# Second FFN matrix converted in blocks of three feature tiles, its last quarter inside the second product; the gMLP's output rows converted in the gMLP

## The chip, the core and the metric

The kernel runs on one core of one Trainium2 chip. The core has TensorE (PE, matmuls and, as PEld, their weight loads), VectorE (DVE), ScalarE (ACT), GpSimd (POOL) and SyncE (SP), which issues all the transfers of this kernel. The metric is device time in microseconds of one execution. Three executions of the kernel before took 1011.33, 1014.9 and 1015.18 us (median 1014.9); a fourth, the profiled one, took 1010.06 us.

## The reference

Attention with capped scores, then a feed-forward layer with layer norm, then a gated MLP (gMLP), for 4 batches of 448 tokens and 768 features (12 heads of 64). The matrices come as 64-bit floats, since each was drawn as 32-bit and scaled by a 64-bit factor. Cut to what is computed:

```python
def _attn_ref(q, k, v, cap):
    scores = cap * np.tanh(scale * (q @ k.T) / cap)
    attn = softmax(scores)
    return attn @ v

def _moe_ref(x, g_ln, w_ch1, w_ch2):                 # w_ch1 768x3072, w_ch2 3072x768
    xn = (x - mu) / np.sqrt(var + 1e-06) * g_ln
    ch = np.maximum(xn @ w_ch1, 0.0) @ w_ch2
    return x + ch

def _moe2_ref(x, w_in, w_spatial, b_spatial, w_out): # w_in 768x1024, w_out 512x768
    h = np.maximum(x @ w_in, 0.0)
    u, v = h[..., :512], h[..., 512:]
    v_n = (v - mean(v)) / np.sqrt(var(v) + 1e-06)
    v_s = np.einsum('ts,bsd->btd', w_spatial, v_n) + b_spatial[None, :, None]
    return (u * v_s) @ w_out
```

## The kernel before

The four batches are worked in two passes, batches 0 and 1 first, then 2 and 3. In the first pass TensorE computes attention for batches 0 and 1 (to about 100 us), then the hidden layer of this pair beside the attention of batches 2 and 3 (`h_units`, 100 to 345 us), then the product with the second feed-forward matrix (`y_seven`, 345 to 497 us) and the gMLP (`gmlp`, from 497 us). The second pass repeats hidden layer, `y_seven` and gMLP for batches 2 and 3.

A matmul in full precision is done as three matmuls with operands split into a high and a low part: `cp` rounds a tile to the high part, `sub` subtracts it to get the low part. Every weight row and every hidden tile goes through this pair of instructions, on ScalarE or VectorE, before TensorE reads it.

Conversion of the matrices. A matrix arrives as pairs of 32-bit words. `value` loads one row of it into a raw tile and makes 32-bit floats in another tile: one ScalarE pass over the upper words (`Prelu` with a power-of-two scale), then either one ScalarE pass over the lower words and one VectorE instruction that joins both (rows of the gMLP, kinds `wv`, `wu`, `wo`), or two VectorE instructions (a shift and a join; kinds `w1`, `w2`). The row is written to DRAM (`kept`), and later uses load the kept copy. For the second matrix (`w2`) a row is one feature tile of one of six groups: 128 partitions x 512 columns, 36 rows. They are converted during the first pass's hidden layer, spread over it by `todo`, with two raw tiles of 512 pairs (`w4`).

`y_seven` computes the second feed-forward product as a 2x2 block product with seven half-size products, in the order 1, 7, 6, 4, 5, 2, 3. Each product runs over six groups; a group is 18 matmuls of 448 columns. `left_block(n, g)` gives the left operand of group g: the quarters of the matrix (a11, a12, a21, a22; three feature tiles by two 128-row tiles, 768 columns a group) come from the kept copy or are formed from others. Product 2's is a12, which product 3 reuses. The left block is split into tile `whm` in groups 0 and 4 and into the ring of three `wh` tiles in the others; there is one `whm`. Hidden tiles `hs` are loaded ahead into ten buffers and split into `rs`.

During products 4, 5 and 2 of the first pass one row of the gMLP's matrices is converted per group (`beside`, `LATER`): six `wv`, four `wu`, six `wo`, with two raw tiles (`w6m`) of 768 pairs and two result tiles (`wcm`).

The order of the work is written by a planner in the kernel itself. The whole program is recorded, each instruction gets a due time from TensorE's position and from the buffers that it frees, and `plan` picks, engine by engine, the ready instruction that is due first, up to `AHEAD` = 28 us ahead of TensorE. The result is one fixed order per engine. On the chip each engine works through its own in that order and waits at an instruction until its inputs and its buffer are there; what stands behind waits too.

Line 553 is the recorder through which nearly all instructions are issued, so tiles, not lines, tell them apart. In names of tiles: `w6m<-in_w_u_dram` is the raw load of a `wu` row, `wcm<-w6m` its first ScalarE pass, `w6m<-w6m` the second (in place over the lower words), `wcm<-wcm,w6m` the VectorE join, `kept_wu<-wcm` the write; `wc<-w` and `kept_w<-wc` belong to rows of the second matrix, `wr<-w` to those of the first (768 columns, converted with the same kinds of instruction); `wqm` and `wqs` hold loaded quarters of the second matrix.

Of the kernel before, what the change touches and what calls it, by code (L numbers as in the profile page):

```python
# [10 lines left out]
F32 = mybir.dt.float32  # L11
F32R = mybir.dt.float32r
I32 = mybir.dt.int32
U32 = mybir.dt.uint32
# [29 lines left out]
FIRST = 2, 7, 2, 10, 2, 2  # L44
# [9 lines left out]
LATER = 4, 5, 2  # L54
# [506 lines left out]
def attn_ffn_gmlp_kernel(  # L561
# [52 lines left out]
    def staged(stage, kind, n, name=None):  # L614
# [14 lines left out]
    w6, es, qks, hx, wc, w4 = (  # L629
        staged(stage, kind, n, name) for (stage, kind, name), n in zip(  # L630
            ((one, "w6", "w6"), (att, "es", "es"), (att, "qk", "qk"), (one, "acc", "hx"), (one, "wq", "wc"),
             (one, "w4", "w4")), FIRST))
# [3 lines left out]
    rbg, vsg, qkg, bsg = (staged(gate, k, n, k + "g") for k, n in (("rb", 8), ("vt", 7), ("qk", 2), ("acc", 1)))  # L636
# [11 lines left out]
    rb, raw6 = [rbg, rb3], [w6, wc, w4]  # L648
# [49 lines left out]
    kept2 = []  # L698
    made = {}
# [8 lines left out]
    def ahead(kind, j):  # L708

        with prog.early():  # L710
            value(kind, j, pool=raw6[1])

    def value(kind, j, home=None, pool=wr):

        n = width[kind]
        if kind == "ws":
            t = hs.get()
            SP.dma_start(out=t, in_=source[kind][j])
        elif (kind, j) in kept:
            t = pool.get()[:, 0:n]  # L720
            SP.dma_start(out=t, in_=kept[kind, j])
        else:
            raw = raw6[0 if n > DH else 2].get()[:, 0:n]
            SP.dma_start(out=raw.rearrange("p n t -> p (n t)"), in_=source[kind][j].bitcast(I32))
            t = pool.get()[:, 0:n]
            ti = t.bitcast(I32)
            hi, lo = raw[:, :, 1], raw[:, :, 0]
            if home is None:
                A.activation(out=t, in_=hi.bitcast(F32), func=ACTF.Prelu, scale=REBASE, alpha=-(2.0 ** 32))
            else:  # L730
                with prog.either():
                    for e in (V, A):
                        if e is A:
                            A.activation(out=t, in_=hi.bitcast(F32), func=ACTF.Copy, scale=REBASE)
                        else:
                            V.tensor_scalar(out=t, in0=hi.bitcast(F32), scalar1=REBASE, scalar2=None, op0=ALU.mult)
            if home is None and kind in ("wv", "wu", "wo"):
                A.activation(out=lo, in_=lo.bitcast(U32), func=ACTF.Copy, scale=TOP, bias=FLOOR)
                V.scalar_tensor_tensor(out=ti, in0=ti, scalar=3, in1=lo, op0=ALU.logical_shift_left,
                                       op1=ALU.bitwise_or)  # L740
            else:
                V.tensor_scalar(out=ti, in0=ti, scalar1=3, scalar2=None, op0=ALU.logical_shift_left)
                if home is not None:
                    V.scalar_tensor_tensor(out=ti, in0=hi, scalar=-(1 << 31), in1=ti, op0=ALU.bitwise_and,
                                           op1=ALU.bitwise_or)
                V.scalar_tensor_tensor(out=ti, in0=lo, scalar=29, in1=ti, op0=ALU.logical_shift_right,
                                       op1=ALU.bitwise_or)
            if kind == "w2":
                if j % KD == 0:
                    kept2.append(dram.tile([128, 2, KD, n // 2], F32, name=f"kept_{kind}_{j}"))  # L750
                SP.dma_start(out=kept2[j // KD][:, :, j % KD], in_=t.rearrange("p (a n) -> p a n", a=2))
            else:
                d = kept[kind, j] = dram.tile([128, n], F32, name=f"kept_{kind}_{j}")
                SP.dma_start(out=d, in_=t)
        return t
# [563 lines left out]
    def gmlp(bs, nxt):  # L1319
# [265 lines left out]
    def y_seven(wq, wqs, beside=()):  # L1585
# [3 lines left out]
        left, right = slice(0, HD), slice(HD, KD)  # L1589
        a11, a12, a21, a22 = ((d, j) for d in (left, right) for j in range(2))  # L1590
# [8 lines left out]
        def left_block(n, g):  # L1599
# [21 lines left out]
            if n == 2:  # L1621
                held["a12", g] = load(a12, g)
                return held["a12", g]
# [115 lines left out]
    def main():  # L1739
# [103 lines left out]
```

## Time and profile before

| | |
|---|---|
| median of three executions | 1014.9 us (1011.33 to 1015.18) |
| profiled execution | 1010.06 us, its span 1008.3 us |
| TensorE busy | 999.5 us, 99% |
| VectorE busy | 868.3 us, 86% |
| ScalarE busy | 580.5 us, 58% |
| granted TensorE clock | 1.00 throughout |
| DMA | 229.05 MB, mean 227 GB/s |

The page gives, for one profiled execution, each engine's busy time; the span runs from the first to the last instruction. Matmuls overlap, so TensorE can be called busy while it runs below its pace; its waits and its order in time say more. Stretches of the span can be asked for one by one. An engine's idle time counts only where another, in the end TensorE, waits for it.

### The profile page before, as it was taken

To read this page: it belongs to the slowest core of one execution; us is meant where nothing else is said; L and a number is where in the kernel's file an instruction comes from. 1 tells how busy PE (TensorE), PEld (TensorE's weight loads), DVE (VectorE), ACT (ScalarE), POOL (GpSimd) and SP (SyncE) were. 2 spreads that over 40 slices of the span, in tenths; PEclk is the share of its full clock that TensorE was granted. 3 is DMA by queue.
4 is the path that set the end of the run, shared out by engine and by line. 5 is a ranking of instruction groups with operands and counts; after the bars stand their busy time and mean duration, and the time that the engine had idled before them with its cause. 6 is when DMAs were issued, how large, how long until landed. Compare 5 with 4: busy or idle time off the path is not lost.

```text
span 1008.3 us, 14836 instructions
## 1 busy us (share of the span) xinstructions
PE 999.5 (99%) x5060; PEld 828.4 (82%) x5060; DVE 868.3 (86%) x1472; ACT 580.5 (58%) x925; POOL 23.0 (2%) x22
## 2 busy tenths in 40 slices
PE   9999999999999999999999999999999999999998
PEld 2332788778778899999989899999999999998987
DVE  6979898878888789999869999877788988968996
ACT  8999776776667347674335355444454542314653
POOL 0000110000000000000001200000000000000010
PEclk9999999999999999999999999999999999999999
DMA  8444779999999999998044143565699867302402
GB/s 282 136 128 146 261 262 366 357 365 356 343 368 361 362 376 323 330 405 276 26 154 141 39 138 122 176 194 191 232 330 375 291 183 233 103 22 71 128 22 110
DMA packets 124848, 229.05 MB, mean 227 GB/s; under 512 B 21170, under 2 KB 93028, under 8 KB 124772
## 3 DMA queue, kind: packets, MB, share of 16 engines
q1 hardware_dynamic: 124772, 228.10, 66.0%
q8 instruction: 40, 0.66, 0.3%
q14 instruction: 36, 0.29, 0.1%
HBM read 157.48 MB, written 70.57 MB: 226 GB/s over the span
## 4 chain that ended last, share of the span: by engine, by line
PE 78%; DMA 11%; DVE 6%; ACT 3%; issue 1%; SPq 1%; DVEq 0%; ACTq 0%
PE bank L553 51%; PE two L553 26%; DMA hs<-inv 3%; DMA w<-in_w_dram 3%; DVE es L553 2%; DMA kept_w<-wc 2%; DMA rc<-sum 1%; ACT es L553 1%; SPq L553 1%; DMA inv<-rc 1%; DVE wr L553 1%; DVE hs L553 1%; ACT hs L553 1%; DMA qk<-in_qk_dram 1%; DVE x L553 1%
## 5 line engine op out<-in xcount | busy, mean ns | idle before, releaser
L553 PE MATMUL bank<-rs,wh 128*128 128x448 f32 x1728 | 361.9, 363 | 0.3 <-ACT hs L553 0.2
L553 PEld LDWEIGHTS bank<-rs,wh 128*128 128x128 f32 x1728 | 322.8, 187 | 27.5 <-issue 4.3
L553 PE MATMUL two<-rs,wh 128*128 128x448 f32 x462 | 103.4, 362 | 0.0
L553 ACT ACTIVATE rs<-hs 128x448 fp32r<-128x448 f32 x137 | 74.6, 570 | 43.0 <-DMA hs<-h 33.2
L553 DVE TENSOR_TENSOR rs<-hs,rs 128x448 fp32r<-128x448 f32 x159 | 94.2, 618 | 1.8 <-ACT rs L553 1.4
L553 PEld LDWEIGHTS two<-rs,wh 128*128 128x128 f32 x462 | 86.6, 187 | 5.8
L553 ACT ACTIVATE es<-es,capt 128x896 f32<-128x896 f32 x72 | 73.1, 1057 | 0.0
L553 ACT ACTIVATE es<-two,qsc 128x896 f32<-128x896 f32 x62 | 60.7, 1017 | 6.8 <-PE two L553 6.6
L553 PE MATMUL bank<-es,vt 128*64 128x448 f32 x288 | 62.2, 552 | 0.0
L553 DVE TENSOR_TENSOR wh<-wr,wh 128x768 fp32r<-128x768 f32 (+2 forms) x66 | 56.3, 856 | 3.8 <-ACT wh L553 3.5
L553 ACT ACTIVATE hs<-bank 128x448 f32<-128x448 f32 x62 | 33.6, 541 | 44.6 <-PE bank L553 34.5
L553 ACT ACTIVATE wh<-wr 128x768 fp32r<-128x768 f32 (+2 forms) x50 | 38.5, 770 | 28.2 <-PE bank L553 15.3
L553 DVE TENSOR_TENSOR es<-es,es 128x896 f32<-128x896 f32 x48 | 51.9, 1081 | 1.8 <-ACT es L553 1.4
L553 PEld LDWEIGHTS bank<-es,vt 128*64 128x64 f32 x288 | 17.4, 136 | 36.9 <-issue 26.7
L553 PE MATMUL two<-qk 64*128 64x448 f32 x168 | 39.9, 580 | 2.0 <-ACT es L553 2.0
L553 ACT ACTIVATE wc<-w 128x512 f32<-128x512 f32 x36 | 24.2, 674 | 30.0 <-DMA kept_w<-wc 13.3
L553 ACT ACTIVATE rs<-x 128x448 fp32r<-128x448 f32 x32 | 18.0, 574 | 37.5 <-DVE x L553 36.1
L553 PEld LDWEIGHTS two<-qk 64*128 64x128 f32 x168 | 14.1, 190 | 27.3 <-ACT es L553 15.4
L553 PE MATMUL two<-wh,rs 128*128 128x512 f32 x144 | 34.7, 390 | 0.0
L553 PE MATMUL bank<-rx,whb 128*128 128x448 f32 x144 | 32.7, 362 | 0.0
L553 PE MATMUL two<-rx,whb 128*128 128x448 f32 x144 | 32.7, 362 | 0.0
L553 DVE TENSOR_SCALAR wc<-wc 128x512 int32<-128x512 int32 x36 | 15.2, 423 | 19.3 <-ACT wc L553 19.0
(249 smaller groups left out, 1878.9 us busy)
## 6 DMA issues: line engine op xcount, KB each, us to landing
hs<-h SPq DMA_DIRECT2D x168, 224.0 KB, 5.2
h<-hx SPq DMA_DIRECT2D x84, 224.0 KB, 5.3
w<-in_w_dram SPq DMA_DIRECT2D x24, 768.0 KB, 6.8
w<-in_w_dram SPq DMA_DIRECT2D x36, 512.0 KB, 6.4
qk<-in_qk_dram SPq DMA_DIRECT2D x24, 448.0 KB, 5.1
h<-hs SPq DMA_DIRECT2D x48, 224.0 KB, 3.7
kept_w<-wr SPq DMA_DIRECT2D x24, 384.0 KB, 7.6
kept_w<-wc SPq DMA_DIRECT2D x36, 256.0 KB, 5.3
```

Of the source, the lines that this page charges most:

```text
L553: fn(*(put(a) for a in args), **{k: put(a) for k, a in kw.items()})
```

## The change

The second matrix is converted by blocks of three feature tiles and half of a group's rows (768 columns, one quarter of one group) in place of rows of 512. A block's raw load reads three pieces of 2 KB per partition, and its kept write is one piece of 3 KB per partition. Three of the four quarters (a11, a21, a22: 18 blocks) are converted during the hidden layer, with one raw tile of 768 pairs (`w6q`) in place of two of 512. The last quarter, a12, is converted block by block where product 2 of the first pass asks for it: raw load into `w6m`, two ScalarE passes and one VectorE join, result in `wqm`, and a kept write for the second pass. The six output rows (`wo`) leave `y_seven` and are converted during the gMLP's gate units, two before each of units 1 to 3, with two raw tiles (`w6g`) and two result tiles (`wqg`) of the gMLP's own stage. The conversion itself becomes a function `convert`, unchanged.

```diff
-FIRST = 2, 7, 2, 10, 2, 2
+FIRST = 2, 7, 2, 10, 2, 1
-LATER = 4, 5, 2
+LATER = 4, 5
...
-             (one, "w4", "w4")), FIRST))
+             (one, "w6", "w6q")), FIRST))
...
-    rbg, vsg, qkg, bsg = (staged(gate, k, n, k + "g") for k, n in (("rb", 8), ("vt", 7), ("qk", 2), ("acc", 1)))
+    rbg, vsg, qkg, bsg, w6g, wcg = (staged(gate, k, n, k + "g") for k, n in (
+        ("rb", 8), ("vt", 7), ("qk", 2), ("acc", 1), ("w6", 2), ("wq", 2)))
...
-    rb, raw6 = [rbg, rb3], [w6, wc, w4]
+    rb, raw6 = [rbg, rb3], [w6, wc, w6q]
...
+    BLOCKS = [(slice(d, d + KD // 2), j) for d in (0, KD // 2) for j in range(2)]
...
     def ahead(kind, j):
 
         with prog.early():
-            value(kind, j, pool=raw6[1])
+            if kind == "w2":
+                block(*j, raw6[1], True)
+            else:
+                value(kind, j, pool=raw6[1])
...
+    def block(q, g, pool, early):
+
+        n = FW // 2
+        raw = raw6[2].get()[:, 0:KD // 2 * n]
+        SP.dma_start(out=raw.rearrange("p (d n) t -> p d (n t)", n=n),
+                     in_=w2[g * KD + q[0].start:g * KD + q[0].stop, :, q[1] * n:q[1] * n + n].bitcast(I32)
+                     .rearrange("d p n -> p d n"))
+        t = pool.get()[:, 0:KD // 2 * n]
+        convert(t, raw, True, not early)
+        if len(kept2) == g:
+            kept2.append(dram.tile([128, 2, KD, n], F32, name=f"kept_w2_{g}"))
+        SP.dma_start(out=kept2[g][:, q[1], q[0]].rearrange("p d n -> p (d n)"), in_=t)
+        return t
+
+    def convert(t, raw, sign, low):
+
+        ti = t.bitcast(I32)
+        hi, lo = raw[:, :, 1], raw[:, :, 0]
+        if sign:
+            A.activation(out=t, in_=hi.bitcast(F32), func=ACTF.Prelu, scale=REBASE, alpha=-(2.0 ** 32))
...
+        if sign and low:
+            A.activation(out=lo, in_=lo.bitcast(U32), func=ACTF.Copy, scale=TOP, bias=FLOOR)
+            V.scalar_tensor_tensor(out=ti, in0=ti, scalar=3, in1=lo, op0=ALU.logical_shift_left,
+                                   op1=ALU.bitwise_or)
+        else:
+            V.tensor_scalar(out=ti, in0=ti, scalar1=3, scalar2=None, op0=ALU.logical_shift_left)
...
             for i in range(1, KH):
+                for k in range(2 * i - 2, 2 * i):
+                    ahead("wo", k)
                 u_units(bs, i)
...
             if n == 2:
-                held["a12", g] = load(a12, g)
+                held["a12", g] = load(a12, g) if last_pass[0] else block(a12, g, wq, False)
                 return held["a12", g]
...
-            rows = [("w2", j) for j in range(NG * KD)]
-            later = [("wv", k) for k in range(KD)] + [("wu", i) for i in range(KH)] + [("wo", k) for k in range(KD)]
+            rows = [("w2", (q, g)) for q in (BLOCKS[0], BLOCKS[2], BLOCKS[3]) for g in range(NG)]
+            later = [("wv", k) for k in range(KD)] + [("wu", i) for i in range(KH)]
...
             raw6[:] = w6m, wcm, w6m
             y_seven(wqm, wqs, later)
+            raw6[:] = w6g, wcg, w6g
             gmlp(bs, [2 * p + 2, 2 * p + 3])
```

The planner runs again over the changed program, so orders move on every engine. Three places follow. In the names, the last number tells buffers apart; `h0_2_4` is the hidden tile 4 of product 2.

SyncE, before, from the kept write of the third gate row on, late in product 5:

```order
L553 DMA kept_wu_2_309<-wcm0_3339 128x768
L553 DMA w6m0_3337<-in_w_out_dram 128x1024
L553 DMA wqm5_3336<-kept_w2_30_267 128x768
L553 DMA hs3_82<-h0_2_8_260 128x448
L553 DMA kept_wu_3_310<-wcm1_3340 128x768
L553 DMA w6m1_3338<-in_w_out_dram 128x1024
L553 DMA hs2_81<-h0_2_9_272 128x448
L553 DMA hs9_88<-h0_2_10_283 128x448
L553 DMA hs5_84<-h0_2_11_294 128x448
L553 DMA hs6_85<-h0_3_0_169 128x448
L553 DMA hs4_83<-h0_3_1_176 128x448
L553 DMA kept_wo_0_311<-wcm0_3339 128x512
```

SyncE now, from the same write on:

```order
L553 DMA kept_wu_2_309<-wcm0_3192 128x768
L553 DMA w6m0_3190<-in_w2_dram 128x3x512
L553 DMA hs8_87<-h0_2_5_228 128x448
L553 DMA hs6_85<-h0_2_6_239 128x448
L553 DMA kept_wu_3_310<-wcm1_3193 128x768
L553 DMA w6m1_3191<-in_w2_dram 128x3x512
L553 DMA hs3_82<-h0_2_7_250 128x448
L553 DMA hs2_81<-h0_2_8_261 128x448
L553 DMA hs0_79<-h0_2_9_272 128x448
L553 DMA w6m0_3190<-in_w2_dram 128x3x512
```

Raw loads of blocks 0, 1 and 2 of the last quarter stand where raw loads of output rows stood, and fewer hidden tiles' loads are ahead of them; the loads of product 2's kept blocks (`wqm<-kept_w2`) are gone.

ScalarE, before, around the conversion of the first output row (`wcm0`) at the end of product 5:

```order
L553 ACTIVATE rs11_74<-hs0_79 128x448
L553 ACTIVATE wh0_94<-wqm2_3333 128x768
L553 ACTIVATE rs13_76<-hs7_86 128x448
L553 ACTIVATE whm0_3342<-wqm0_3331 128x768
L553 ACTIVATE wcm0_3339<-w6m0_3337 128x512
L553 ACTIVATE rs14_77<-hs8_87 128x448
L553 ACTIVATE w6m0_3337<-w6m0_3337 128x512
L553 ACTIVATE rs15_78<-hs1_80 128x448
```

ScalarE now, around the blocks 0 to 2 (`wqm0` to `wqm2`) of the last quarter:

```order
L553 ACTIVATE wqm0_3184<-w6m0_3190 128x768
L553 ACTIVATE w6m0_3190<-w6m0_3190 128x768
L553 ACTIVATE rs12_75<-hs7_86 128x448
L553 ACTIVATE rs13_76<-hs1_80 128x448
L553 ACTIVATE rs14_77<-hs4_83 128x448
L553 ACTIVATE wqm1_3185<-w6m1_3191 128x768
L553 ACTIVATE rs15_78<-hs9_88 128x448
L553 ACTIVATE w6m1_3191<-w6m1_3191 128x768
L553 ACTIVATE rs0_63<-hs5_84 128x448
L553 ACTIVATE wqm2_3186<-w6m0_3190 128x768
L553 ACTIVATE w6m0_3190<-w6m0_3190 128x768
L553 ACTIVATE whm0_3195<-wqm0_3184 128x768
```

The two passes over block 2 stand ahead of the split of block 0 into `whm0`, which product 2's first group reads. Before, VectorE made that split, from the loaded kept block, and ScalarE none of it.

VectorE now, at the end of the gMLP's first product, between the splits of the last `wv` row and the first two `wu` rows:

```order
L553 TENSOR_TENSOR wh0_94<-wr1_93,wh0_94 128x512
L553 SCALAR_TENSOR_TENSOR wqg0_4307<-wqg0_4307,w6g0_4305 128x512
L553 SCALAR_TENSOR_TENSOR wqg1_4308<-wqg1_4308,w6g1_4306 128x512
L553 CAST wh1_95<-wr0_92 128x768
L553 TENSOR_TENSOR wh1_95<-wr0_92,wh1_95 128x768
L553 SCALAR_TENSOR_TENSOR wqg0_4307<-wqg0_4307,w6g0_4305 128x512
L553 CAST wh2_96<-wr1_93 128x768
L553 TENSOR_TENSOR wh2_96<-wr1_93,wh2_96 128x768
L553 SCALAR_TENSOR_TENSOR wqg1_4308<-wqg1_4308,w6g1_4306 128x512
```

Four joins of output rows (`wqg`) stand there; before, this place held none.

## Rows read from the trace of the kernel before

**Rows 1.** The page: busy time of each engine, its share, and instructions:

```profile
PE 999.5 (99%) x5060; PEld 828.4 (82%) x5060; DVE 868.3 (86%) x1472; ACT 580.5 (58%) x925; POOL 23.0 (2%) x22
```

**Rows 2.** Stretches; the first line names the columns, then clock, DMA share, GB/s:

```profile
core 0: us, PE busy (x) PEld busy (x) DVE busy (x) ACT busy (x) POOL busy (x), PEclk, DMA share, GB/s
100.00:345.00 245.00, 244.53 (x1344) 190.49 (x1341) 208.03 (x339) 172.59 (x253) 8.62 (x2) 1.00 0.96 338
432.00:454.00 22.00, 22.00 (x112) 20.63 (x111) 21.36 (x31) 15.85 (x26) 0.00 (x0) 1.00 1.04 405
454.00:475.00 21.00, 21.00 (x107) 19.68 (x106) 18.81 (x31) 10.39 (x19) 0.00 (x0) 1.00 0.92 299
497.00:527.00 30.00, 30.00 (x135) 24.93 (x134) 21.94 (x39) 10.72 (x20) 0.00 (x0) 1.00 0.37 119
527.00:560.00 33.00, 33.00 (x167) 30.62 (x167) 32.20 (x71) 19.91 (x39) 2.54 (x2) 1.00 0.41 136
```

**Rows 3.** What TensorE waited for between 100 and 345 us, and how often:

```profile
PE bank L553 <- ACT hs L553: 0.2, 1, 0.2
PE bank L553 <- DVE wh L553: 0.2, 1, 0.2
```

**Rows 4.** Groups of instructions: form and count | busy us, mean ns | idle before:

```profile
L553 DVE SCALAR_TENSOR_TENSOR wr<-w,wr 128x768 int32<-128x768 int32 x28 | 26.4, 952 | 0.1
...
L553 DVE SCALAR_TENSOR_TENSOR wc<-w,wc 128x512 int32<-128x512 int32 x36 | 24.5, 684 | 0.1
L553 ACT ACTIVATE wc<-w 128x512 f32<-128x512 f32 x36 | 24.2, 674 | 30.0 <-DMA kept_w<-wc 13.3 <-DMA w<-in_w_dram 12.8 <-DVE acc L553 2.2
...
L553 ACT ACTIVATE wr<-w 128x768 f32<-128x768 f32 x20 | 17.6, 909 | 4.8 <-DMA kept_w<-wr 2.9 <-DVE es L553 1.4 <-DMA w<-in_w_dram 0.5
...
L553 DVE TENSOR_SCALAR wc<-wc 128x512 int32<-128x512 int32 x36 | 15.2, 423 | 19.3 <-ACT wc L553 19.0
...
L553 DVE TENSOR_SCALAR wr<-wr 128x768 int32<-128x768 int32 x24 | 13.1, 551 | 0.7 <-ACT wr L553 0.5
...
L553 DVE SCALAR_TENSOR_TENSOR wcm<-wcm,w6m 128x512 int32<-128x512 int32 x12 | 8.2, 687 | 0.8 <-ACT w6m L553 0.7
```

**Rows 5.** SyncE's issues in order of time: start us, us, what:

```profile
419.28 0.38 SPq L553 DMA_DIRECT2D w6m<-in_w_u_dram  x1
...
429.74 0.32 SPq L553 DMA_DIRECT2D kept_wu<-wcm  x1
430.16 0.38 SPq L553 DMA_DIRECT2D w6m<-in_w_u_dram  x1
...
441.54 0.32 SPq L553 DMA_DIRECT2D kept_wu<-wcm  x1
442.14 0.33 SPq L553 DMA_DIRECT2D w6m<-in_w_out_dram  x1
```

**Rows 6.** ScalarE in order of time; in brackets the idle time before:

```profile
426.55 0.93 ACT L553 ACTIVATE wcm<-w6m 128x768 f32<-128x768 f32 x1 [2.92 <-DMA w6m<-in_w_u_dram]
...
427.83 0.89 ACT L553 ACTIVATE w6m<-w6m 128x768 int32<-128x768 uint32 x1
...
437.19 0.92 ACT L553 ACTIVATE wcm<-w6m 128x768 f32<-128x768 f32 x1 [1.00 <-DMA w6m<-in_w_u_dram]
```

**Rows 7.** VectorE in order of time:

```profile
428.76 0.96 DVE L553 SCALAR_TENSOR_TENSOR wcm<-wcm,w6m 128x768 int32<-128x768 int32 x1 [1.35 <-ACT w6m L553]
...
451.04 0.56 DVE L553 CAST whm<-wqm 128x768 fp32r<-128x768 f32 x1 [0.37 <-PE bank L553]
```

**Rows 8.** TensorE in order of time around the start of product 2:

```profile
447.44 3.76 PE L553 MATMUL bank<-rs,whm 128*128 128x448 f32 x18
...
454.64 2.56 PE L553 MATMUL two<-rs,whm 128*128 128x448 f32 x12
```

**Rows 9.** Tile w6m between 400 and 480 us: its DMAs:

```profile
DMA to landing us min/median/max: 4.4/6.1/7.2
```

**Rows 10.** Issues by size, KB each, median us to landing:

```profile
w6m<-in_w_u_dram SPq DMA_DIRECT2D x4, 768.0 KB, 7.0
```

More of the change, by code (lines that the diff above doesn't have):

```diff
@@ L628, in attn_ffn_gmlp_kernel @@
     three = Stage(prog, tc, "three", (four,))
-    w6, es, qks, hx, wc, w4 = (
+    w6, es, qks, hx, wc, w6q = (
         staged(stage, kind, n, name) for (stage, kind, name), n in zip(
             ((one, "w6", "w6"), (att, "es", "es"), (att, "qk", "qk"), (one, "acc", "hx"), (one, "wq", "wc"),
-             (one, "w4", "w4")), FIRST))
+             (one, "w6", "w6q")), FIRST))
     vts = [staged(att, "vt", 1, f"vt{i}_") for i in range(2)]
@@ L722, in value @@
         else:
-            raw = raw6[0 if n > DH else 2].get()[:, 0:n]
+            raw = raw6[0].get()[:, 0:n]
             SP.dma_start(out=raw.rearrange("p n t -> p (n t)"), in_=source[kind][j].bitcast(I32))
             t = pool.get()[:, 0:n]
[L726 to L736, printed above, removed]
@@ L737, in value @@
-            if home is None and kind in ("wv", "wu", "wo"):
-                A.activation(out=lo, in_=lo.bitcast(U32), func=ACTF.Copy, scale=TOP, bias=FLOOR)
-                V.scalar_tensor_tensor(out=ti, in0=ti, scalar=3, in1=lo, op0=ALU.logical_shift_left,
-                                       op1=ALU.bitwise_or)
[L741 to L755, printed above, removed]
+            convert(t, raw, home is None, kind in ("wv", "wu", "wo"))
@@ new lines, in value @@
+            d = kept[kind, j] = dram.tile([128, n], F32, name=f"kept_{kind}_{j}")
+            SP.dma_start(out=d, in_=t)
+        return t
[10 more added lines that the diff above has]
+        SP.dma_start(out=kept2[g][:, q[1], q[0]].rearrange("p d n -> p (d n)"), in_=t)
+        return t
@@ new lines, in convert @@
+    def convert(t, raw, sign, low):
[4 more added lines that the diff above has]
+        else:
+            with prog.either():
+                for e in (V, A):
+                    if e is A:
+                        A.activation(out=t, in_=hi.bitcast(F32), func=ACTF.Copy, scale=REBASE)
+                    else:
+                        V.tensor_scalar(out=t, in0=hi.bitcast(F32), scalar1=REBASE, scalar2=None, op0=ALU.mult)
+        if sign and low:
+            A.activation(out=lo, in_=lo.bitcast(U32), func=ACTF.Copy, scale=TOP, bias=FLOOR)
+            V.scalar_tensor_tensor(out=ti, in0=ti, scalar=3, in1=lo, op0=ALU.logical_shift_left,
+                                   op1=ALU.bitwise_or)
+        else:
+            V.tensor_scalar(out=ti, in0=ti, scalar1=3, scalar2=None, op0=ALU.logical_shift_left)
+            if not sign:
+                V.scalar_tensor_tensor(out=ti, in0=hi, scalar=-(1 << 31), in1=ti, op0=ALU.bitwise_and,
+                                       op1=ALU.bitwise_or)
+            V.scalar_tensor_tensor(out=ti, in0=lo, scalar=29, in1=ti, op0=ALU.logical_shift_right,
+                                   op1=ALU.bitwise_or)
@@ L1588, in y_seven @@
         HD = KD // 2
-        left, right = slice(0, HD), slice(HD, KD)
-        a11, a12, a21, a22 = ((d, j) for d in (left, right) for j in range(2))
+        a11, a12, a21, a22 = BLOCKS
         held = {}
```

## The prediction

> **What bounds the kernel now.** I read the page first, then stretches of the span, then the waits of single engines, and last the engines in order of time around the work that moves. TensorE is busy for 999.5 of 1008.3 us [rows 1]. That figure alone proves little, because matmuls overlap, so I looked at what TensorE waited for. From 100 to 345 us, where the first pair's hidden layer is made beside attention and where the second matrix (called w2 below) is converted today, it is busy for 244.53 of 245.00 us at a granted clock of 1.00 [rows 2], and its named waits come to 0.4 us [rows 3]. In the products of that matrix, and in the gMLP behind them, it is busy for all of 432 to 454, 454 to 475, 497 to 527 and 527 to 560 us [rows 2]. The reader is to see two things. Time taken off VectorE, ScalarE or the DMA queue can give back almost nothing, since TensorE hardly waits for them. And any wait that the change puts in front of TensorE is added whole, because no later stretch shown has idle time to absorb it.
>
> **The hidden-layer stage.** Today 36 rows of 512 columns are converted there: VectorE 0.423 + 0.684 us each, 39.9 us, and ScalarE 0.674 us each, 24.3 us. Afterwards 18 blocks of 768 columns are: VectorE 0.551 + 0.952 us, 27.1 us, and ScalarE 0.909 us, 16.4 us [rows 4]. That is 12.8 us of VectorE and 7.9 us of ScalarE less. Raw reads fall from 36 x 512 KB to 18 x 768 KB and kept writes from 36 x 256 KB to 18 x 384 KB, 7.1 MB less to move. What it gives is bounded by the 0.5 us that TensorE idles there [rows 2]. The second raw tile goes away. One block's turn, at the 10.4 us that a 768-column conversion takes from issue to its last VectorE instruction (419.28 to 428.76 + 0.96) [rows 5, 7], makes 188 us for 18 blocks in a stage of 245 us, and a held SyncE has hidden tiles loaded ahead as cover; if that cover is gone, one late block costs a few us. I take 0, between -0.5 and +2.
>
> **Product 2 of the first pair.** This is the term that decides. Today its left block is loaded from the kept copy, and the raw tiles are turning over gate and output rows that nobody waits for. Afterwards each of its six blocks is read raw, converted by two ScalarE passes and one of VectorE, and only then split for TensorE. The two raw tiles are the same pair as before, and they are still busy with gate rows when block 0 wants one. In the order of SyncE block 0's load stands right behind the kept write of the third gate row, exactly where the first output row's load stands today, at 442.14 us, held by that write at 441.54 [rows 5]. In the order of ScalarE the split of block 0 (tile whm) stands behind both passes over block 2, because whm is not free until product 5's fifth group has been read: VectorE waits for TensorE before it fills whm at 451.04 [rows 7]. So TensorE's first group of product 2, which begins at 454.64 today [rows 8], needs block 2 to have landed, and block 2's load waits until block 0 has left the raw tile.
>
> Step by step, with the median landing of these raw loads, 6.1 us [rows 9]: block 0 is issued at 442.1 and lands at 448.2. From ScalarE's start on a 768-column row to the end of VectorE's last instruction on it takes 3.2 us (426.55 to 429.72) [rows 6, 7], so it is converted at 451.4. Block 2 is issued then, lands at 457.6, and has ScalarE's two passes, 0.93 + 0.89 us [rows 6], until 459.4. The split of block 0 follows: about 0.9 us of ScalarE (a pass of the same size) and 0.95 us of VectorE (0.952 for a 768-column instruction [rows 4]), ready at 461.3. That is 6.6 us late against 454.64. Blocks 3 to 5 come at the same pace, and groups of 18 matmuls take 3.6 us, so behind a start that is 6.6 us late none of them is late again. The wait is added once. While ScalarE stands at block 2, the hidden tiles' splits queue behind it; VectorE stands at the blocks' last instruction, and SyncE at block 2's load with later hidden tiles behind it, all needed after the first group.
>
> Bounds: at the landing seen just before ScalarE began on a gate row, 7.3 us (419.28 to 426.55) [rows 5, 6], the same sum gives 463.6 and 9.0 us late; at the shortest, 4.4 us [rows 9], 457.9 and 3.2 us. It becomes 0 if block 0 also starts some 3 us sooner, which its earlier place among the hidden tiles' loads allows once the gate rows turn faster: the six kept loads of this product leave the queue (2.4 MB; at the 405 GB/s of 432 to 454 us [rows 2] that is 5.8 us of transfer), and five of them lie beside the gate rows. The third gate row needed 7.0 us to land (430.16 to 437.19) [rows 5, 6]. I take 6.6, since the median lies between busy and quiet landings and the traffic falls only before block 0.
>
> The rule that speaks against this is in the Trainium skill, DMA: Bandwidth & Descriptors, section "Anatomy of one DMA — SWDGE (gpsimd) path": a transfer costs about 2.0 us plus its bytes at 436 GB/s, fitted to another issuing path than the one used here. By it a 768 KB load is an estimated 3.8 us, and the wait in product 2 would come to about 2 us. The trace does not agree: 768 KB took 7.0 us in the median [rows 10].
>
> **The gMLP.** Six output rows' conversions move here, 0.687 us of VectorE each [rows 4], 4.1 us, and two ScalarE passes each. From 527 to 560 VectorE is busy for 32.20 of 33.00 us [rows 2], so the end of the normalisation could slip by 3.3 us. But the order puts four of the six ahead of the normalisation's first instruction, into the stretch before, 497 to 527, where VectorE idles for 8.1 us [rows 2]; the two that stay are 1.4 us against 0.8 idle. I take 0, between 0 and +3.3. The kept output rows are read some 30 us after they are written, behind the spatial product.
>
> **Sum.** 1010.06 us of the profiled execution (1008.3 of span and 1.8 around it) + 6.6 = 1016.7. The four executions shown run from 1010.06 to 1015.18 with a mean of 1012.9 and a median of 1014.9 for the three unprofiled ones. On the mean the same 6.6 gives 1019.5, which I predict; on the median 1021.5, +0.65%.
>
> **Rivals.** First, the wait is hidden. Without the kept loads the gate rows turn faster, block 2 lands by 451 and product 2 starts on time. For it: SyncE's order has block 0 three hidden tiles earlier than the output row it replaces, and landings go down to 4.4 us [rows 9]. Against it: the queue stays at 0.92 to 1.04 of its engines' time in both products [rows 2], and the bytes of product 2 with raw blocks are as many as before. Time: 1012.9, at most 3 us more. The formula of the Trainium skill named above points here. Second, faster: the place is 150 to 345 us, where the queue is full (0.96 over the whole stage [rows 2]); the slower executions of the kernel before may be those in which late transfers hold TensorE there, and 7.1 MB less, 21 us of transfer at 338 GB/s, would bring all of them to the profiled one's 1010. It decides once TensorE's waits there exceed 5 us in an ordinary execution. Against it stand the 0.4 us [rows 3]. Third, more: the long landing of 9.0 us and the gMLP's 3.3 together, 12.3, which gives 1025.2; it needs VectorE's surplus to reach TensorE.
>
> **Chances and range.** Forecast (3 to 9 us more) 0.48, hidden 0.30, faster 0.12, more 0.10. What a measurement of this kernel can tell from no change is 0.5%, 5.1 us. About 0.36 of the forecast's 0.48 lies above that, and with the third rival slower has 0.46; faster has 0.12; the rest, 0.42, is within. The range reaches down to the profiled time less the 0.5 us of the first stage, 1009.5, and up to 1027, where the third rival meets the slowest execution shown (1015.2 + 12.3). The forecast's own range is 1015 to 1023.
>
> **What would show it.** Right: TensorE idles once, just ahead of product 2's first group, for 3 to 9 us, with whm on ScalarE behind a pass that waited for a raw w2 load; busy stretches before and after are unchanged. Wrong: no gap there (then the landings are short, or block 0 went out before 439), a gap at the fifth group instead, or a gap at the spatial product (then VectorE in the gMLP is the price). If the span falls by over 3 us, TensorE waited for the queue in the hidden-layer stage more than this trace shows.

## The result, and the profile after

The changed kernel takes 1019.8 us in the median of 7 runs (1016.09 to 1023.89), the kernel before 1012.17 us (7 runs, 1009.99 to 1015.18): a ratio of 1.0079, 95% interval 1.006 to 1.0098. The profiled execution of the changed kernel took 1021.44 us, its span 1019.7 us.

The page again says that TensorE is busy all the time (answer to [rows 1]):

```profile
PE 1004.7 (99%) x5060; PEld 829.6 (81%) x5060; DVE 866.7 (85%) x1447; ACT 580.0 (57%) x912; POOL 25.1 (2%) x24
```

The stretches of [rows 2], now (columns as there):

```profile
100.00:345.00 245.00, 242.85 (x1329) 187.99 (x1326) 200.06 (x309) 162.66 (x230) 7.87 (x2) 1.00 0.90 313
432.00:454.00 22.00, 21.59 (x109) 19.90 (x108) 18.80 (x27) 13.15 (x19) 0.00 (x0) 1.00 0.91 316
454.00:475.00 21.00, 17.83 (x80) 15.88 (x79) 17.42 (x29) 11.44 (x18) 0.00 (x0) 0.92 0.99 351
497.00:527.00 30.00, 30.00 (x141) 25.98 (x140) 24.44 (x47) 10.44 (x19) 0.00 (x0) 1.00 0.33 102
527.00:560.00 33.00, 33.00 (x161) 29.91 (x160) 29.00 (x63) 18.00 (x33) 1.32 (x1) 1.00 0.77 278
```

TensorE idles 2.1 us in the hidden layer (0.5 before), where VectorE and ScalarE are less busy and the DMA queue moves less (0.90 of its time for 0.96). It idles over 3 us in product 2, at a lower granted clock.

**Lag.** Both kernels issue 5060 matmuls, in one order but for a stretch of the gMLP (from 561 to 600 us), so the start of the same matmul in two traces says how far one is behind. The table has that lag against the profile before, in us, added in each stretch (bounds in the time of the kernel before). The changed kernel was profiled three times; the last three lines are two other kernels (below) that have its order of instructions on every engine until past the last block of the hidden layer. The stretch 432–499 holds products 5 and 2.

| profiled execution | to 130 | 130–343 | 343–432 | 432–499 | 499–601 (gMLP) | behind | end |
|---|---|---|---|---|---|---|---|
| changed, first | 0.5 | 2.9 | 0.0 | 6.0 | 0.9 | 1.1 | 11.4 |
| changed, second | −0.9 | 3.2 | 0.0 | 2.5 | 1.7 | 1.3 | 7.8 |
| changed, third | 0.4 | 6.1 | 0.8 | 2.6 | 1.1 | 1.0 | 12.0 |
| gate rows beside products 6 and 4 | 1.0 | 8.3 | 0.0 | 0.4 | 0.6 | 1.4 | 11.7 |
| the same, again | 0.3 | 5.9 | 0.0 | 0.0 | 0.6 | 1.4 | 8.2 |
| other tile in product 2 | 0.8 | 9.8 | 0.0 | 2.5 | 3.2 | 0.8 | 17.1 |

The profile before was one of the quick executions, so lags at the end exceed the 7.6 us between the medians.

Not all of the stretch 432–499 is product 2. The changed kernel loses 0.7, 0.5 and 0.7 us of it at the first group of product 5, where TensorE waits for VectorE's part of whm (0.9 us with the other tile, 0.4 and 0.0 us in the two lines with earlier gate rows). First profile:

```profile
437.43 3.48 PE L553 MATMUL bank<-rs,whm 128*128 128x448 f32 x16 [0.41 <-DVE whm L553]
```

That leaves 5.3, 2.0 and 1.9 us for product 2 in the three profiles.

**Product 2.** SyncE's raw loads of blocks 0, 1 and 2, then ScalarE, then TensorE in order of time, changed kernel, first profile (answer to [rows 8]):

```profile
440.50 0.78 SPq L553 DMA_DIRECT2D w6m<-in_w_dram  x1
445.43 0.47 SPq L553 DMA_DIRECT2D w6m<-in_w_dram  x1
450.56 0.38 SPq L553 DMA_DIRECT2D w6m<-in_w_dram  x1
```

```profile
447.56 0.92 ACT L553 ACTIVATE wqm<-w6m 128x768 f32<-128x768 f32 x1 [1.91 <-DMA w6m<-in_w_dram]
...
458.57 0.89 ACT L553 ACTIVATE wqm<-w6m 128x768 f32<-128x768 f32 x1 [3.90 <-DMA w6m<-in_w_dram]
459.36 0.87 ACT L553 ACTIVATE w6m<-w6m 128x768 int32<-128x768 uint32 x1
460.12 0.83 ACT L553 ACTIVATE whm<-wqm 128x768 fp32r<-128x768 f32 x1
```

```profile
455.14 3.76 PE L553 MATMUL bank<-rs,wh 128*128 128x448 f32 x18
461.01 0.68 PE L553 MATMUL two<-rs,whm 128*128 128x448 f32 x2 [2.11 <-ACT whm L553]
462.75 3.85 PE L553 MATMUL two<-rs,whm 128*128 128x448 f32 x10 [1.06 <-DVE whm L553]
466.44 1.36 PE L553 MATMUL bank<-rs,whm 128*128 128x448 f32 x6
```

Block 0 was in place at 450.5, but its split (whm, 460.12) stands behind both passes over block 2, whose load went out at 450.56 and on which ScalarE could begin 8.0 us later. TensorE waits 2.11 us for the high part and 1.06 us for VectorE's low part. The ten matmuls behind take 3.85 us. In the second profile ScalarE began on block 2 6.6 us after its load went out, the waits came to 1.4 us, and the same ten matmuls take 2.28 us:

```profile
457.93 0.67 PE L553 MATMUL two<-rs,whm 128*128 128x448 f32 x2 [0.35 <-ACT whm L553]
459.66 2.28 PE L553 MATMUL two<-rs,whm 128*128 128x448 f32 x10 [1.06 <-DVE whm L553]
```

**Hidden layer.** There are two places. At 300 us ScalarE stands 4.15 us at its first pass over a block, whose raw load goes out only after the block before has left the one raw tile. The pass that empties TensorE's bank (`hs<-bank`) is next behind it; TensorE waits 0.66 + 0.23 us, since its banks come free one by one. ScalarE, then TensorE, first profile:

```profile
302.00 0.90 ACT L553 ACTIVATE wc<-w6q 128x768 f32<-128x768 f32 x1 [4.15 <-DMA w6q<-in_w_dram]
302.80 0.52 ACT L553 ACTIVATE hs<-bank 128x448 f32<-128x448 f32 x1
```

```profile
303.37 0.47 PE L553 MATMUL bank<-rs 64*128 64x448 f32 x1 [0.66 <-ACT hs L553]
304.08 0.47 PE L553 MATMUL bank<-rs 64*128 64x448 f32 x1 [0.23 <-DVE hs L553]
```

At 185 us it is a row of the first matrix: ScalarE waits until an earlier row has been written to its kept copy and its buffer is free, with `hx<-bank` behind it, and TensorE waits for hx:

```profile
185.67 0.91 ACT L553 ACTIVATE wr<-w 128x768 f32<-128x768 f32 x1 [2.96 <-DMA kept_w<-wr]
186.49 0.53 ACT L553 ACTIVATE hx<-bank 128x448 f32<-128x448 f32 x1
```

```profile
187.07 0.47 PE L553 MATMUL bank<-rs 64*128 64x448 f32 x1 [1.26 <-ACT hx L553]
```

Before, no conversion of ScalarE between 180 and 187 us, or between 296 and 303 us, waited more than 0.5 us. The planner ordered both stretches anew with the changed conversions. Tile w6q over the whole kernel: counts of its users with first and last start, and who waited for it, us and times:

```profile
L553 ACT ACTIVATE wc<-w6q x18: 882/912/937, 95.6 to 311.6; 128x768 f32<-128x768 f32 x18
...
  ACT wc L553: 12.9, 9
```

Eighteen passes from 95.6 to 311.6 us make 12.7 us a turn.

What the two places cost differs with the clock granted behind the waits. Over the stretch 135 to 345 us it was 1.00, 1.00, 0.99, 0.98, 0.99 and 0.98 in the six executions of the table, in its order, and the losses there go with it: 2.9 and 3.2 us at 1.00, 5.9 and 6.1 at 0.99, 8.3 and 9.8 at 0.98. By an estimate from these figures (210 us times what is missing from 1.00) the clock took up to 2 and 4 us of them. The first and the third profile at 300 us (columns as in [rows 2]):

```profile
300.00:310.00 10.00, 9.11 (x58) 6.72 (x52) 4.77 (x8) 7.82 (x11) 0.00 (x0) 1.00 0.93 298
300.00:310.00 10.00, 8.32 (x46) 5.17 (x45) 4.58 (x8) 6.37 (x10) 0.00 (x0) 0.83 0.96 288
```

### The profile page after: what moved, and what is told of

Its sections match the earlier page's. It is cut to its first block, busy times and chain, and to the rows that moved or that the text cites. A ratio compares the mean times of both kernels' runs of the same rounds, so it can differ in the third digit from the quotient of the medians.

```text
span 1019.7 us, 14692 instructions
## 1 busy us (share of the span) xinstructions
PE 1004.7 (99%) x5060; PEld 829.6 (81%) x5060; DVE 866.7 (85%) x1447; ACT 580.0 (57%) x912; POOL 25.1 (2%) x24
## 4 chain that ended last, share of the span: by engine, by line
PE 73%; DMA 15%; DVE 5%; ACT 4%; issue 2%; SPq 1%; POOL 0%; DVEq 0%; ACTq 0%
PE bank L553 49%; PE two L553 24%; DMA h<-hx 3%; ACT es L553 2%; DMA hs<-inv 2%; DMA w6m<-in_w_v_dram 2%; DMA hs<-h 1%; DMA w6m<-in_w_u_dram 1%; DMA wqm<-kept_w 1%; DMA wqs<-kept_w 1%; DVE rs L553 1%; ACT hs L553 1%; DVE es L553 1%; DMA w6m<-in_w_dram 1%; DMA w6q<-in_w_dram 1%
## 5 line engine op out<-in xcount | busy, mean ns | idle before, releaser
L553 ACT ACTIVATE rs<-hs 128x448 fp32r<-128x448 f32 x131 | 71.8, 570 | 48.0 <-DMA hs<-h 46.3
L553 ACT ACTIVATE hs<-bank 128x448 f32<-128x448 f32 x58 | 31.5, 543 | 43.3 <-PE bank L553 42.8
L553 ACT ACTIVATE wh<-wr 128x768 fp32r<-128x768 f32 (+2 forms) x44 | 33.8, 770 | 21.8 <-DVE wr L553 11.7
L553 ACT ACTIVATE hx<-bank 128x448 f32<-128x448 f32 x33 | 17.8, 540 | 27.5 <-PE bank L553 27.2
L553 PEld LDWEIGHTS two<-wh,rs 128*128 128x128 f32 x144 | 27.0, 188 | 5.5
```

The lines of the kernel that those rows point to most:

```text
L553: fn(*(put(a) for a in args), **{k: put(a) for k, a in kw.items()})
```

## The experiments

Ratios are against the kernel before, run on the same chip beside them. The first four undo, mend or isolate one part each.

**All four quarters in the hidden layer.** Product 2's loads are the kept ones again.

```diff
-            rows = [("w2", (q, g)) for q in (BLOCKS[0], BLOCKS[2], BLOCKS[3]) for g in range(NG)]
+            rows = [("w2", (q, g)) for q in (BLOCKS[0], BLOCKS[2], BLOCKS[3], BLOCKS[1]) for g in range(NG)]
...
-                held["a12", g] = load(a12, g) if last_pass[0] else block(a12, g, wq, False)
+                held["a12", g] = load(a12, g)
```

> The changed kernel, with the last quarter's six blocks also converted in the hidden layer (24 blocks through the one raw tile) and loaded from the kept copy in product 2, as before. Theory A (the cost is one place: the split of block 0 into whm stands on ScalarE behind the passes over block 2, which wait for that block's raw load; 3.2 us of waiting and about 2 us of half clock behind it, some 6 of the 8 us): product 2 starts at most 0.5 us later than its place 20 us before it gives, its granted clock stays 1.00, and the ratio to the kernel before falls from 1.008 to 1.002 (1.000 to 1.004). Rival H (the hidden layer with a single raw tile and its new order is the cost): six more blocks go through that tile, TensorE's lag at 345 us grows beyond the 3.5 us seen in the changed kernel, and the ratio stays at 1.007 or more.

Measured: 1033.41 us, ratio 1.0208 (1.0187 to 1.0228). What product 2 cost went (0.0 us in that stretch), but 15.2 us were lost between 343 and 432 us. The tile view of w6q, then TensorE in product 6:

```profile
L553 ACT ACTIVATE wc<-w6q x24: 885/894/919, 96.4 to 391.3; 128x768 f32<-128x768 f32 x24
...
  ACT wc L553: 38.9, 19
```

```profile
407.65 6.86 PE L553 MATMUL bank<-rs,whm 128*128 128x448 f32 x18 [6.88 <-ACT whm L553]
```

At 12.8 us a turn 24 blocks last until 391 us, some 40 us past the hidden layer, and SyncE's loads of the quarter that product 6 reads go out from 399.03 us, behind the last block's write at 394.36. For product 2 theory A held, its ratio missed. Rival H's ratio came from another place than it said: the lag at 345 us was 5.7 us, inside the changed kernel's own spread (2.3 to 6.6). One raw tile has no room in the hidden layer for many more than 18 blocks.

**Another tile for the split.** Groups 0 and 4 of product 2 use the wh ring.

```diff
-                w = (wh if n in (1, 7) or g % 2 or g % 4 and not last_pass[0] else
+                w = (wh if n in (1, 7) or g % 2 or (g % 4 or n == 2) and not last_pass[0] else
```

> The changed kernel, with the left blocks of product 2's groups 0 and 4 (first pass) split into the ring of three wh tiles in place of the one whm. In ScalarE's order the split of block 0 then stands ahead of the passes over blocks 1 and 2; loads, raw tiles and conversions are unchanged. Theory A: the first group of product 2 starts on time (within 1 us), and with it the 6 us go: ratio 1.002 (1.000 to 1.004). Rival P (the pair of raw tiles is too slow whatever stands first): blocks come every 5.5 us (raw loads at 440.5, 445.4, 450.6, 455.2, 461.2, 467.3 us in the changed kernel) while a group takes 3.6 us, so an early start makes the last blocks late instead: block 5, issued at 467.3, lands 7 us later and needs 3 us more, 477, against a last group that would begin at 454.6 + 18 = 472.7; TensorE then waits some 4 us before groups 3 to 5 and the ratio is 1.005 to 1.008.

Measured: 1021.26 us, 1.009 (1.0062 to 1.0117). TensorE in order of time, around product 2's start and near its end:

```profile
462.51 3.76 PE L553 MATMUL bank<-rs,wh 128*128 128x448 f32 x18
466.11 2.56 PE L553 MATMUL two<-rs,wh 128*128 128x448 f32 x12
...
499.26 0.37 PE L553 MATMUL two<-rs,wh 128*128 128x448 f32 x1
500.22 2.48 PE L553 MATMUL two<-rs,wh 128*128 128x448 f32 x11 [0.59 <-DVE rs L553]
```

Product 2 starts without a wait, with the same loads: the order of ScalarE made the first wait. Some of it comes back from 481 us on (1.6 us of lag), less than the 4 us of rival P. The time did not fall: this execution lost 9.8 us in the hidden layer, whose order is the changed kernel's, and 3.2 us in the gMLP. So theory A held for the first group and missed the ratio.

**Output rows in the gMLP alone**, in the kernel before:

```diff
             for i in range(1, KH):
+                for k in range(2 * i - 2, 2 * i):
+                    ahead("wo", k)
                 u_units(bs, i)
```

(with w6g and wcg as in the change, LATER = 4, 5, and no `wo` in `later`.)

> The kernel before with one part of the change alone: the six output rows converted in the gMLP, two before each of gate units 1 to 3, with raw and result tiles of that stage; the second matrix is converted by rows of 512 and loaded as before. Theory A: this part costs about the 1 us by which the changed kernel falls back further between 497 and 600 us; ratio 1.001 (0.999 to 1.003). Rival G (VectorE's surplus in the gMLP reaches TensorE, the 3.3 us bound of the prediction, and the clock falls there too): ratio 1.004 or more, and a wait of TensorE for VectorE between 527 and 600 us.

Measured: 1015.07 us, 1.0038 (1.0022 to 1.0054): between theory and rival G. Its profile loses 3.3 us between 499 and 601 us, behind VectorE as rival G has it, though at full clock and later than 560. TensorE there:

```profile
566.43 0.47 PE L553 MATMUL bank<-rs,onesr 128*128 128x448 f32 x1 [1.04 <-DVE rs L553]
...
573.16 0.47 PE L553 MATMUL bank<-rs,onesr 128*128 128x448 f32 x1 [0.52 <-DVE rs L553]
...
587.17 3.08 PE L553 MATMUL bank<-rs,wh 128*128 128x448 f32 x14 [0.62 <-DVE rs L553]
```

**Gate rows a product earlier**, twice; the second time beside the changed kernel on one chip.

```diff
-LATER = 4, 5
+LATER = 6, 4
```

> The changed kernel, with the ten gate rows converted beside products 6 and 4 in place of products 4 and 5, so that the raw pair is free a product earlier and block 0's raw load no longer stands behind the third gate row's kept write. The blocks are still read raw and converted for product 2. Theory A: blocks 0 and 1 are converted in product 5, product 2 starts within 1 us of its time, ratio 1.002 (1.000 to 1.004). Rival P: blocks 2 to 5 still go through the pair at 5.5 us each; the start of 0 and 1 some 15 us sooner covers that, so 1.002 here too, but 1.005 or more where only the order of the split is mended. Rival R (the raw bytes themselves, 4.7 MB read and 2.4 MB written beside hidden tiles on a full queue, delay the hidden tiles): ratio 1.005 or more, and TensorE waits for rs tiles in products 6 to 2.

> The kernel with gate rows beside products 6 and 4 once more, on one chip with the changed kernel. Up to 345 us both have one order of instructions on every engine, so they differ only behind it. Theory B: product 2 starts on time here and 2.4 to 6 us late in the changed kernel, so its median is 2 to 5 us below the changed kernel's, ratio to the kernel before 1.003 (1.001 to 1.006); its lag at 345 us is of the changed kernel's size on the same chip. Rival N (the two trade off: what product 2 gives back is lost again, in hidden tiles or the gMLP): both medians within 1.5 us of each other, ratio 1.006 or more.

> The changed kernel once more, beside the others on the same chip. Theory B: ratio 1.008 (1.006 to 1.010) again; in its profile product 2 starts 4 to 7 us late against the hidden layer's lag, and that lag at 345 us lies anywhere between 2 and 10 us, since the raw loads' landings differ from execution to execution. If the lag in the hidden layer is 9 us here and product 2's 6 come on top, single profiles of this kernel differ by up to 6 us from that place alone.

> The changed kernel, a third time, for the comparison with the run above on one chip. Theory B: ratio 1.007 (1.005 to 1.010), with 2 to 4 us late in the hidden layer (at 185 and 300 us) and 2.4 to 6 us in product 2. Rival N: ratio as above, within 0.0015 of the other kernel's.

Measured: 1018.61 us, 1.0062 (1.0039 to 1.0085), and 1017.45 us, 1.0048 (1.0026 to 1.0071). The changed kernel in the later runs: 1017.77 us, 1.0061 (1.0046 to 1.0075), and, beside the second, 1019.75 us, 1.0074 (1.0044 to 1.0103). TensorE, first profile of this kernel:

```profile
460.79 3.76 PE L553 MATMUL bank<-rs,wh 128*128 128x448 f32 x18
464.39 2.56 PE L553 MATMUL two<-rs,whm 128*128 128x448 f32 x12
```

The wait ahead of product 2 is gone in both profiles (0.4 and 0.0 us in that stretch, the 0.4 at product 5), and nothing takes its place up to 600 us, against rivals R and N; the first ratio still misses theory A's 1.000 to 1.004. The medians on one chip differ by 2.3 us, the size of the 2.5 us that the stretch 432–499 cost in two of the three profiles, but the intervals overlap: by time alone the gain is not settled, by the traces the wait is. What is left is mostly the hidden layer, 8.3 and 5.9 us here. For the changed kernel the ratios came as expected, but not the places: product 2 lost 2.0 us in the second profile (4 to 7 expected) and 1.9 in the third (2.4 to 6), and the hidden layer 6.1 in the third (2 to 4).

**The hidden layer's raw tile.** Three ways to have more than one. Two tiles, with the rings hx and hs cut from 10 to 9; one ring of three shared with the first matrix's rows; two raw tiles and one result tile, with the gate rows beside 6 and 4. And the cut rings with one raw tile as a control.

```diff
 # two raw tiles, rings of 9 (third run: also LATER = 6, 4; fourth run: one raw tile, FIRST ends in 1)
-COUNTS = 16, 10, 3, 2, 3, 1
-FIRST = 2, 7, 2, 10, 2, 1
+COUNTS = 16, 9, 3, 2, 3, 1
+FIRST = 2, 7, 2, 9, 2, 2
 # one ring of three
-FIRST = 2, 7, 2, 10, 2, 1
+FIRST = 3, 7, 2, 10, 2, 0
-    rb, raw6 = [rbg, rb3], [w6, wc, w6q]
+    rb, raw6 = [rbg, rb3], [w6, wc, w6]
 # two raw tiles, one result tile, rows beside 6 and 4
-FIRST = 2, 7, 2, 10, 2, 1
+FIRST = 2, 7, 2, 10, 1, 2
-LATER = 4, 5
+LATER = 6, 4
```

> The changed kernel with two raw tiles of 768 pairs for the second matrix's blocks in the hidden layer in place of one; to make room the hidden tiles' write buffers hx go from 10 to 9 and the load buffers hs from 10 to 9. Theory B (two places cost: in the hidden layer, at about 185 and 300 us, ScalarE stands at its first pass over a block, which waits for the one raw tile's load, 4.45 us in the run with the other tile, and the activations behind it that empty TensorE's banks come late; and product 2's start): TensorE's lag against the kernel before at 345 us falls to 1.5 us or less (3.5 in the changed kernel, 9.4 and 10.6 in the last two runs), the start of product 2 stays some 6 us late, ratio 1.004 (1.001 to 1.006). Rival S (the lag of the hidden layer comes from the blocks' longer instructions and the new order, not from the tile): lag at 345 us of 3 us or more, waits for hs or hx as before, ratio 1.007 or more.

> The changed kernel with the same memory used otherwise: the two raw tiles of the first matrix's rows and the one of the blocks become one ring of three, from which both kinds take in turn; all other buffers as in the changed kernel. Theory B: a block's load no longer waits for the block before it but for the third raw load back, so ScalarE's idle time ahead of the blocks' first passes shrinks below 2 us at any one, the lag at 345 us falls to 2 us or less, product 2 stays late, ratio 1.004 (1.001 to 1.007). Rival S: lag at 345 us of 3 us or more, ratio 1.007 or more; a ring that couples both kinds could also add a wait for the first matrix's rows (wh), and then the ratio exceeds 1.009.

> Both places mended: two raw tiles for the blocks in the hidden layer (hx and hs at 9) and the gate rows converted beside products 6 and 4, so that blocks 0 and 1 are ready before product 2. Theory B: both lags go, what stays is 1 to 3 us in the gMLP; ratio 1.001 (0.998 to 1.004). Rival S: 1.004 or more from the hidden layer alone.

> The changed kernel with hx and hs at 9 buffers each and still one raw tile: the control for the two runs with two raw tiles, which lost 20 us. Theory B: the smaller rings cost it, above all behind 600 us, where those two runs fell back by 7 us and more at the second pass's first rows; ratio 1.015 to 1.022, with the 300 us wait for the raw tile back. Rival Q (the second raw tile itself costs, by filling the queue ahead of other loads): ratio 1.008 to 1.011, no loss behind 600 us.

> Gate rows beside products 6 and 4, two raw tiles for the blocks in the hidden layer, and one result tile in place of two to make room (a block's first pass then waits until the block before it is written to its kept copy). Other buffers as in the changed kernel. Theory B: the load wait at 300 us goes, a wait for the kept write may stand in its place, about as long as a write of 384 KB takes; ratio 1.004 (1.001 to 1.009). If the raw tile were all, 1.002; if one result tile is as bad as one raw tile, 1.006 or more.

Lag is again that of the n-th matmul. TensorE's order differs in these kernels between 113 and 143 us, in those with rings of 9 also from 89 to 106 and from 560 to 610 us, so two neighbouring columns can trade up to 1 us. From 343 to 432 us the second line lost 0.8 us, the others nothing.

| | ratio (95%) | to 130 | 130–343 | 432–499 | gMLP | behind |
|---|---|---|---|---|---|---|
| two raw, rings of 9 | 1.0218 (1.0197 to 1.024) | 5.3 | 4.4 | 2.9 | 0.2 | 8.6 |
| the same, rows beside 6 and 4 | 1.0193 (1.0176 to 1.0209) | 3.5 | 5.3 | 0.0 | 0.1 | 8.9 |
| control: one raw, rings of 9 | 1.0261 (1.023 to 1.0293) | 7.2 | 11.0 | 2.8 | 0.7 | 7.5 |
| ring of three | 1.0093 (1.0073 to 1.0112) | 4.4 | 0.9 | 1.8 | 1.1 | 0.6 |
| two raw, one result, 6 and 4 | 1.0049 (1.003 to 1.0069) | 2.7 | 5.9 | 0.0 | 0.6 | 1.4 |

Only the last lies inside what theory B gave, and the lags at 345 us (9.7, 8.8 and 5.4 us for two raw tiles, the same with earlier rows, and the ring of three) are as rival S had them, though 3.5 to 5.3 us of each arose before 130 us. The control names one reason: all three kernels with rings of 9 lose 7.5 to 8.9 us behind 600 us, where the changed kernel loses 1.1. That has nothing to do with the blocks; whether it is the smaller rings or the other order of TensorE there is not told apart. In the control, at the second pass's first rows:

```profile
634.46 0.47 PE L553 MATMUL bank<-rs,whb 128*128 128x448 f32 x1 [1.70 <-ACT rs L553]
636.67 1.11 PE L553 MATMUL bank<-rs,whb 128*128 128x448 f32 x2 [1.74 <-DVE rs L553]
```

Between the control and two raw tiles at the same rings, the second tile is worth 6.6 us between 130 and 343 us (one profile each) and 4.3 thousandths of ratio (in two sets of runs, whose intervals overlap). The ring of three leaves 0.9 us there: 0.3 us of waiting is left at the place of 185 us and none at that of 300. But each kernel with more raw tiles, and the control too, is late at 124 to 128 us, for example in the ring of three:

```profile
123.55 0.97 PE L553 MATMUL bank<-qk 64*64 64x448 f32 x4
126.98 1.42 PE L553 MATMUL bank<-qk 64*64 64x448 f32 x4 [2.46 <-DMA qk<-in_qk_dram]
```

This load has nothing to do with the blocks, and it did not go out late: at 123.66 us, against 123.52 in the kernel before and 124.00 in the changed one. What moved is TensorE's own order. The eight matmuls stand 18 us later there, behind the groups of `rs,rs` and `rs,wh`; in the kernel before:

```profile
141.74 0.98 PE L553 MATMUL bank<-qk 64*64 64x448 f32 x8
```

With one result tile the wait at 300 went too. The place at 185 us cost 5.5 us, a wait of 2.31 us and a lower clock behind it, and ScalarE's passes over the blocks waited for the kept write instead:

```profile
  DMA kept_w<-wc: 7.5, 6
```

So more than one raw tile takes away the wait at 300 us: it is absent in all four such kernels and there in the control (1.65 us of TensorE; the block's load went out at 309.45 us, ScalarE began on it at 317.55). No variant that fits the memory was free of another wait. No version beat the kernel before.

## Why the prediction came out as it did

**The total** was forecast at 1019.5 and measured at 1019.8 us, inside the forecast's own range (1015 to 1023) and slower by more than 0.5%, the likeliest of the three cases by a little. Against before it is 7.6 us where 6.6 was written. The working behind it was half right: one term came out smaller, two others were not nothing.

**Product 2, +6.6 (3.2 to 9.0, or 0 with an earlier start).** The mechanism is the one described, link by link: block 2's load behind block 0's conversion, both passes over it, the split of whm behind them, no later group late. TensorE waits twice, for the high and for the low part. The size was 5.3, 2.0 and 1.9 us: two of three lie under the sum at the shortest landing, and the idle time of 3 to 9 us that was to show the forecast right is there in the first profile alone (3.2 us; 1.4 in the others). The mis-sized terms are the start and the landing. Block 0's load went out at 440.50, 439.26 and 443.71 us, with TensorE 4.1, 2.8 and 8.0 us late in front of product 2, so some 6 us sooner in TensorE's time than the 442.1 taken; the possibility was named (gate rows turn faster without the kept loads) and not taken. The landing of 6.1 us [rows 9] was misread: that median mixes gate rows of 768 KB with output rows of 512 KB, and the shortest, 4.4 us, is an output row's:

```profile
w6m<-in_w_out_dram SPq DMA_DIRECT2D x6, 512.0 KB, 4.4
```

The blocks are of 768 KB, for which [rows 10] has 7.0 us. ScalarE began on blocks 0 and 2 7.1 and 8.0 us after their loads went out in the first profile, 6.9 and 6.6 in the second, 7.5 and 6.6 in the third. With each profile's own start and these times the sum of the prediction gives 3.7, 2.2 and 2.1 us, and TensorE's start lost 3.6, 2.0 and 2.0. In the first profile another 1.6 us were no wait at all but slow matmuls, a price the working had not. Nor had it the 0.5 to 0.7 us at product 5's first group, whose cause was not looked for.

The ScalarE piece shown of before in the section on the change is not the place its caption names: it is the split of a quarter at product 4's first group beside the first wv row. The place that the change alters is VectorE's split of whm at 451.04 [rows 7], and the argument rests on that.

The rule of the Trainium skill (DMA: Bandwidth & Descriptors, "Anatomy of one DMA — SWDGE (gpsimd) path") that made 3.8 us of a 768 KB load an estimate is again not what the trace shows: 7.0 us in the median of the gate rows, which are of that size. By it the wait would have been about 2 us, near two of the profiles, for the wrong reason: the earlier start made it small, not the landing; with the start as it was that estimate leaves no wait.

**Hidden layer, 0 (−0.5 to +2).** This step failed. 2.9, 3.2 and 6.1 us were lost there in the changed kernel, and up to 9.8 under the same order; the clock behind the waits, which the working had not, is in the larger ones. The argument that the gain is bounded by the 0.5 us that TensorE idles there was right and says nothing of what can be lost. The turn was taken from one gate row (10.4 us) and is 12.7. The cover named (hidden tiles loaded ahead) protects TensorE's inputs; what came late was its outputs, banks that ScalarE empties behind a pass that waits for a load. That one late block costs a few us if that cover is gone stood in the text, and was left out of the sum.

**gMLP, 0 (0 to 3.3).** 0.9 to 1.7 us in the changed kernel, 3.3 us and 0.38% (0.22% to 0.54%) alone: within the bounds, at the upper one alone, and VectorE is the price as the third rival said. A further 1.0 to 1.3 us behind 600 us was not foreseen; its cause was not looked for.

**Rivals.** Hidden (1012.9): refuted for this kernel by the wait in all three profiles, though in two of them product 2 lost only 2 us. Faster through fewer bytes: the queue did fall from 0.96 to 0.90 in the hidden layer, and TensorE idled more, not less. More (1025.2): its VectorE part is real and smaller, its long landing was seen once (8.0 us for block 2).

**Sum.** In the first profile 0.5 + 2.9 + 6.0 + 0.9 + 1.1 = 11.4 us over the span of 1008.3. The medians differ by 7.6, since the profile before was quick and the changed kernel's runs spread over 8 us. That the number was met is in part luck: product 2 came out 1.3 to 4.7 us smaller than its term, the hidden layer 2.9 to 6.1 larger than nothing, and the rest came to 2.6 to 4.0 us.

## What to carry to other kernels

A buffer that is cut from two to one has to be costed by its whole turn, taken from the stage's slowest rows, and by what stands behind its waiting reader on that engine, passes that empty banks included. "No idle time here" bounds what a change can give and not what it can take: a stage without slack needs a term of its own. Where a planner writes the order, expect each edit to make some unrelated wait, and judge by several profiles: one order lost 2.9 us in one execution and 9.8 us in another, where the clock fell behind two of its waits.

## What the runs showed of the hardware

TensorE's granted clock falls behind short waits, and stays low when work is there again. First profile of the changed kernel, product 2's start (columns as in [rows 2]):

```profile
454.00:458.00 4.00, 4.00 (x22) 3.75 (x21) 3.73 (x7) 0.67 (x2) 0.00 (x0) 1.00 0.98 326
458.00:462.00 4.00, 1.58 (x7) 0.81 (x5) 1.74 (x4) 3.13 (x4) 0.00 (x0) 1.00 1.03 401
462.00:466.00 4.00, 3.25 (x9) 2.91 (x10) 3.64 (x7) 2.31 (x4) 0.00 (x0) 0.61 0.99 322
```

Behind 3.2 us of waits with two matmuls between them the clock is 0.61 for 4 us, a mean of its two levels (1.2 and 2.4 GHz), and ten matmuls take 3.85 us that took 2.28 in the second profile, where the waits were 1.4 us and the clock stayed at 1.00. In the kernel with gate rows beside 6 and 4, waits of 1.47 and 0.23 us at 306 us among short matmuls were followed by the lower level:

```profile
306.38 0.46 PE L553 MATMUL bank<-rs 64*128 64x448 f32 x1 [1.47 <-ACT hs L553]
```

```profile
304.00:308.00 4.00, 2.30 (x16) 1.52 (x12) 2.08 (x4) 2.99 (x5) 0.00 (x0) 0.85 0.98 339
308.00:312.00 4.00, 4.00 (x12) 3.14 (x10) 1.49 (x3) 4.00 (x6) 0.00 (x0) 0.50 0.85 238
```

The lag grew there by 5.4 us for 1.7 us of waits, in product 2 above by 5.3 for 3.2. A longer wait in the second profile left the clock at 1.00:

```profile
186.53 0.47 PE L553 MATMUL bank<-rs 64*128 64x448 f32 x1 [2.12 <-ACT hx L553]
```

```profile
188.00:192.00 4.00, 4.00 (x22) 3.75 (x21) 3.24 (x5) 4.00 (x6) 0.00 (x0) 1.00 1.04 366
```

So a wait can cost 1.7 to 3 times its length, and whether it does is not told by its length alone. It differs between executions: runs of the kernel with gate rows beside 6 and 4 at a mean clock of 1.00 took 1013.5 to 1013.9 us, those at 0.995 took 1021.1 to 1021.9.
